# Loading the first K block by partitions (16, then 112) in rows of 64 KB, and writing the last head apart, in a decode attention kernel

## The chip, the cores and the metric

The kernel runs on one core of one Trainium2 chip; the other cores are idle. The metric is the device time of one execution in microseconds (us).

HBM is the chip's main memory and SBUF the core's own, of 128 rows called partitions. A load is issued on the queue of an engine and cut into packets, here one row each, which 16 DMA engines carry side by side (in the kernel before, the first 16 packets all start between 1.74 and 2.10 us).

## The reference

It is one decoding step of grouped-query attention: 32 query heads, 8 K/V heads, one query position, 65,536 keys, head size 128, all in bf16.

```python
B, Hq, Hkv, Sq, Sk, D = 1, 32, 8, 1, 65536, 128

def reference(q, k, v):
    rep = Hq // Hkv                       # 4 query heads share a K/V head
    k = jnp.repeat(k, rep, axis=1)
    v = jnp.repeat(v, rep, axis=1)
    scores = jnp.einsum("bhqd,bhkd->bhqk", q, k) * D ** -0.5
    p = _softmax(scores, axis=-1)
    return jnp.einsum("bhqk,bhkd->bhqd", p, v)
```

K and V are 128 MiB each and every byte is used once, so the kernel is a stream of loads with arithmetic beside it.

## The kernel before

K and V are cut into 16 blocks of 8 MiB each (block i is half of a head). A block lies in SBUF as 128 partitions of 64 KB; partition p holds 256 consecutive keys, a single run of 64 KB in HBM. There are two K buffers and one V buffer. All blocks are loaded on the queue of SP (SyncE), in the order K0, K1, V0, K2, V1, K3, V2, ...

```python
FIRST = (64, 64, 128)     # columns (keys per partition) of the pieces of K0
KLAST = (128, 128)
VLAST = (72, 32, 16, 8)

def src(t, i):
    h, c = divmod(i, C)
    return t[h, c * CK:(c + 1) * CK, :].rearrange("(p t) d -> p (t d)", p=P)

# on SP
def load(buf, t, i, a, b, s):
    sp.dma_start(buf[:, a * D:b * D], src(t, i)[:, a * D:b * D]).then_inc(s, 16)

def load_k(i):
    if i >= NK:                                   # NK = 2 buffers
        sp.wait_ge(tr_s, (i - NK + 1) * G)        # block i-2 transposed
    if i in (0, N - 1):
        for n, a, b in pieces(FIRST if i == 0 else KLAST):
            load(kbuf[i % NK], kf, i, a, b, (first_in if i == 0 else klast_in)[n])
    else:
        load(kbuf[i % NK], kf, i, 0, T, k_in[i % NK])

def load_v(i):
    if i < N - HALVED:
        if i >= 1:
            sp.wait_ge(pv_s, 2 * i)               # products with block i-1 done
        load(vbuf, vf, i, 0, T, v_in)
        return
    # ... the last two V blocks in pieces

load_k(0)
for j in range(1, N + 1):
    if j < N:
        load_k(j)
    load_v(j - 1)
sp.wait_ge(ox_s, 1)
sp.dma_start(of.rearrange("h (a i) -> a h i", a=A), oX).then_inc(o_out, 16)   # all heads
sp.wait_ge(o_out, 16)
```

q (8 KB) is loaded four times, one copy for every 32 partitions, from the queue of ScalarE (ACT), at the same time as the first K loads:

```python
# on ACT
for a in range(A):                                # A = 4
    ac.dma_start(q4[a * S4:(a + 1) * S4, :], qf).then_inc(q_in, 16)
```

VectorE (DVE) waits for q, spreads it, and transposes a K block in 16 pieces; TensorE (PE) makes scores of each piece; ACT moves the scores out of PSUM and takes the exponentials. The products with V block i follow the scores of K block i+1. V1 can be loaded only after K0 and K1 have been transposed, one after the other, and V0 has been used.

## Time and profile before

The median is 628.71 us (6 runs, 628.66 to 628.82).

| Reading | Value | From |
|---|---|---|
| DMA | 9 tenths busy or more in 39 of 40 slices | slices |
| VectorE, TensorE, ACT | 54, 43, 44% busy | busy times |
| packet of 64 KB / 32 KB / 16 KB, one engine | 2.418 / 1.213 / 0.611 us | packet records of the trace |
| block of 8 MiB, steady | 19.35 us | 8 packets of 64 KB on each of 16 engines |

The page's slices of the kernel before (each digit the busy share of a fortieth of the span in tenths, GB/s what the DMA moved):

```profile
span 627.5 us, 20255 instructions
...
DVE  2949176390853908448094470935719367195900
...
DMA  9999999999999999999999999999999999999996
GB/s 368 439 456 414 455 414 455 414 451 414 451 418 451 418 451 418 443 426 434 434 426 439 418 451 409 460 409 460 409 460 409 460 409 460 409 428 434 434 432 276
```

The DMA row is what bounds the kernel: 32 blocks at 19.35 us are 619 us of the 627.5. The packet records, which give the start, length, size and queue of every packet, have no gap to speak of on any of the 16 engines (0.3 us of idle per engine in all) from the first packet at 1.74 us to the end of the last loads at 622.5 to 624.1 us. In such a stream DMA time that is lost is lost for good (below, a first block that lands 19.8 us late ends in a last one 21.3 us late), and work on other engines counts only where it makes the queue run dry (6.2 us in k_whole below).

The windows view of the first 50 us (busy time of each engine in the stretch, then granted clock, DMA share and GB/s; packets of 64 KB make neighbouring stretches uneven, and shares can pass 1):

```profile
core 0: us, PE busy (x) PEld busy (x) DVE busy (x) ACT busy (x) POOL busy (x), PEclk, DMA share, GB/s
0.00:10.00 10.00, 0.00 (x0) 0.00 (x0) 0.29 (x2) 1.49 (x2) 0.67 (x6) 1.00 0.85 331
10.00:20.00 10.00, 2.61 (x73) 2.26 (x74) 7.83 (x15) 1.05 (x5) 0.00 (x0) 1.00 1.06 452
20.00:30.00 10.00, 4.45 (x126) 3.79 (x122) 8.52 (x9) 5.81 (x28) 0.00 (x0) 1.00 1.08 469
30.00:40.00 10.00, 2.46 (x67) 2.03 (x64) 5.74 (x8) 6.86 (x32) 0.30 (x1) 1.00 0.98 420
40.00:50.00 10.00, 2.48 (x68) 2.13 (x69) 6.28 (x6) 4.18 (x14) 0.07 (x1) 1.00 0.97 420
```

Some lines of its timeline (start, length, engine, line, operation, operands; in brackets the idle time before it and what ended it), and how long the q loads took to land, from the view of that tensor:

```profile
12.01 0.24 DVE L290 STREAM_TRANSPOSE scs<-scs 128x64 int32<-128x64 int32 x1 [10.85 <-DMA scs<-in_q_dram]
...
71.19 0.33 SPq L126 DMA_DIRECT2D vbuf<-in_v_dram  x1
...
625.03 0.16 DVE L386 TENSOR_TENSOR oTX<-acc,small 128x4 bf16<-128x4 f32 x1 [11.91 <-PE acc L212]
625.23 0.21 DVE L388 STREAM_TRANSPOSE oTX<-oTX 128x32 bf16<-128x32 bf16 x1
625.47 0.67 SPq L158 DMA_DIRECT2D out_dram<-oTX  x1
...
DMA to landing us min/median/max: 4.1/7.8/9.9
```

VectorE waits 10.85 us for q, not for K. V1 is issued at 71.19 us, while the engines are busy with the block queued before it until 80.0 to 81.8 us, so 8.8 to 10.6 us remain. The tail from the last accumulate at 625.03 us to the end is 2.5 us.

### The profile page before, as it was taken

The page shows a single profiled execution, that of the slowest core. Times are in us where ns is not written, and L with a number is a line of the kernel's source. Part 1 is how long each engine was busy: PE and PEld are TensorE (multiplying, and loading weights), DVE is VectorE, ACT ScalarE, POOL GpSimd, SP SyncE. Part 2 cuts the span into 40 slices and gives each one's busy share as a digit, 9 for nine tenths or more (in the row PEclk, how much of TensorE's full clock was granted, in tenths as well). Part 3 has the DMA queues.
Part 4 walks back from the last instruction along what each step waited for, and adds up shares of the span by engine and source line. Part 5 has one row for each costly group of instructions (what it writes and reads, how often), then busy time and mean ns, then how long its engine had stood idle before and what let it go on. Part 6 is the DMA issues. An engine that isn't in the chain of part 4 may idle for free.

```text
span 627.5 us, 20255 instructions
## 1 busy us (share of the span) xinstructions
PE 267.3 (43%) x8194; PEld 241.6 (39%) x8194; DVE 341.3 (54%) x411; ACT 274.8 (44%) x1178; POOL 10.5 (2%) x32
## 2 busy tenths in 40 slices
PE   0414537154361543615346252462624526146445
PEld 0314426044361433614335152351524525146444
DVE  2949176390853908448094470935719367195900
ACT  0556435164351734517346172451625526264640
POOL 0000000000000000000000000000000000000000
DMA  9999999999999999999999999999999999999996
GB/s 368 439 456 414 455 414 455 414 451 414 451 418 451 418 451 418 443 426 434 434 426 439 418 451 409 460 409 460 409 460 409 460 409 460 409 428 434 434 432 276
DMA packets 6088, 268.53 MB, mean 428 GB/s; under 512 B 964, under 2 KB 964, under 8 KB 1220
## 3 DMA queue, kind: packets, MB, share of 16 engines
q1 hardware_dynamic: 5892, 268.45, 99.1%
q10 hardware_dynamic: 192, 0.03, 0.0%
q8 instruction: 2, 0.03, 0.0%
q14 instruction: 2, 0.02, 0.0%
HBM read 268.47 MB, written 0.01 MB: 428 GB/s over the span
## 4 chain that ended last, share of the span: by engine, by line
DMA 66%; DVE 15%; PE 9%; issue 9%; SPq 1%; DVEq 0%
DMA kbuf<-in_k_dram 58%; DVE ktb L303 14%; PE acc L212 9%; DMA vbuf<-in_v_dram 7%; DVE small L310 1%; PE qkb L203 1%; SPq L126 1%; DVEq L354 0%; DVEq L356 0%; DVE oTX L388 0%; DVE oTX L386 0%; DVEq L385 0%
## 5 line engine op out<-in xcount | busy, mean ns | idle before, releaser
L303 DVE STREAM_TRANSPOSE ktb<-kbuf 128x1024 int32<-128x1024 int32 x256 | 296.0, 1215 | 148.9 <-DMA kbuf<-in_k_dram 148.9
L403 ACT ACTIVATE scs<-qkb 32x64 f32<-32x64 f32 x1024 | 219.5, 214 | 274.9 <-PE qkb L203 263.8
L203 PE MATMUL qkb<-qblk,ktb 128*128 x4096 | 152.2, 175 | 340.3 <-DVE ktb L303 311.0
L203 PEld LDWEIGHTS qkb<-qblk,ktb 128*128 128x128 bf16 x4096 | 129.2, 105 | 363.1 <-DVE ktb L303 363.1
L212 PE MATMUL acc<-pts,vbuf 128*128 128x4 bf16 x4096 | 114.7, 166 | 17.3 <-DMA vbuf<-in_v_dram 12.9
L212 PEld LDWEIGHTS acc<-pts,vbuf 128*128 128x128 bf16 x4096 | 112.0, 104 | 20.1 <-issue 10.6
L310 DVE TENSOR_REDUCE small<-scs 128x4 f32<-128x256 f32 x64 | 36.8, 575 | 61.3 <-ACT scs L403 61.3
L426 ACT ACTIVATE pts<-scs,small 128x256 bf16<-128x256 f32 x64 | 48.9, 853 | 36.8 <-PE acc L212 36.5
L173 POOL PARTITION_ALL_REDUCE small<-small x16 | 5.9, 370 | 588.5 <-DVE small L365 588.5
L426 ACT ACTIVATION_READ_ACCUMULATOR pts<-scs,small 128x1 f32 x64 | 13.7, 214 | 0.0
L372 DVE COPY small<-acc 128x4 f32<-128x4 f32 x8 | 1.3, 163 | 22.7 <-PE acc L212 22.7
L414 ACT ACTIVATE small<-small 128x4 f32<-128x4 f32 x16 | 3.3, 206 | 22.4 <-POOL small L173 22.4
L378 DVE TENSOR_TENSOR small<-acc,small 128x4 f32<-128x4 f32 x7 | 1.1, 162 | 15.7 <-PE acc L212 15.7
L386 DVE TENSOR_TENSOR oTX<-acc,small 128x4 bf16<-128x4 f32 x1 | 0.2, 163 | 11.9 <-PE acc L212 11.9
L290 DVE STREAM_TRANSPOSE scs<-scs 128x64 int32<-128x64 int32 x1 | 0.2, 245 | 10.9 <-DMA scs<-in_q_dram 10.9
L365 DVE TENSOR_REDUCE small<-small 128x4 f32<-128x16 f32 (+1 forms) x16 | 2.9, 184 | 1.3
L165 POOL PARTITION_ALL_REDUCE small<-small x8 | 3.4, 430 | 12.7 <-DVE small L323 12.7
L370 DVE TENSOR_TENSOR small<-small 128x4 f32<-128x4 f32 x8 | 1.3, 163 | 4.0 <-POOL small L173 4.0
L321 DVE TENSOR_TENSOR small<-small 128x4 f32<-128x4 f32 x8 | 1.3, 164 | 3.0 <-ACT pts L426 2.7
L396 ACT ACT_TABLE_LOAD x1 | 1.3, 1283 | 3.0 <-issue 3.0
L381 DVE TENSOR_TENSOR oTX<-small 128x4 f32 x7 | 1.1, 164 | 1.7 <-DVE small L327 1.7
L319 DVE TENSOR_TENSOR small<-small 128x4 f32<-128x4 f32 x8 | 1.4, 180 | 0.9
(18 smaller groups left out, 8.8 us busy)
## 6 DMA issues: line engine op xcount, KB each, us to landing
kbuf<-in_k_dram SPq DMA_DIRECT2D x3, 4096.0 KB, 39.8
vbuf<-in_v_dram SPq DMA_DIRECT2D x3, 4096.0 KB, 24.5
kbuf<-in_k_dram SPq DMA_DIRECT2D x2, 2048.0 KB, 11.0
vbuf<-in_v_dram SPq DMA_DIRECT2D x1, 2304.0 KB, 11.2
vbuf<-in_v_dram SPq DMA_DIRECT2D x1, 1024.0 KB, 13.3
vbuf<-in_v_dram SPq DMA_DIRECT2D x1, 512.0 KB, 14.1
vbuf<-in_v_dram SPq DMA_DIRECT2D x1, 256.0 KB, 14.3
kbuf<-in_k_dram SPq DMA_DIRECT2D x14, 49.4
```

What stands on the lines that cost most here:

```text
L126: sp.dma_start(buf[:, a * D:b * D], src(t, i)[:, a * D:b * D]).then_inc(s, 16)
L165: g.partition_all_reduce(lsum, rhead, P, bass.bass_isa.ReduceOp.add).then_inc(ls_s, 1)
L173: g.partition_all_reduce(mtot if b else mfirst, hmax[:, b * R:(b + 1) * R], P, bass.bass_isa.ReduceOp.max,).then_inc(hma_s, 1)
L203: ins = pe.matmul(o, lhsT=kt[:, be // NE, be % NE, n * P:(n + 1) * P], rhs=q_, start=be == 0, stop=be == NB * NE - 1,)
L212: ins = pe.matmul(acc[:, 0:R], lhsT=vbuf[:, t * D:(t + 1) * D], rhs=pts[:, t * R:(t + 1) * R], start=t == 0, stop=t == T - 1,)
L303: dv.transpose(to.rearrange("p (b t j) -> p b t j", b=NB, t=TG), fr.rearrange("p (t b i) -> p b t i", b=NB, t=TG),).then_inc(tr_s, 1)
L310: dv.tensor_reduce(hp[b][:, u * R:(u + 1) * R], scs[:, u * W:(u + 1) * W].rearrange("p (n g) -> p g n", g=R), AX.X, ALU.max,).then_inc(mx_ ...
L319: dv.tensor_tensor(o2, o1, wgt, ALU.mult).then_inc(ow_s, 1)
L365: dv.tensor_reduce(hmax[:, b * R:(b + 1) * R], hp[b].rearrange("p (u g) -> p g u", g=R), AX.X, ALU.max,).then_inc(hm_s, 1)
L403: ins = ac.activation(to[a * S4:(a + 1) * S4, x, :, :], fr[x * S4:(x + 1) * S4, a, :, :], AF.Copy)
L414: ac.activation(negb[b], mtot if b else mfirst, AF.Copy, scale=-scale).then_inc(nb_s, 1)
L426: ac.activation(pv[:, g_, :], sv[:, g_, :], AF.Exp, bias=negb[b][:, g_:g_ + 1], scale=scale, accum_out=rsum[b][:, g_:g_ + 1],).then_inc(ex ...
```

## The change

The intent is twofold: to read the first K block in whole rows of 64 KB instead of pieces of rows, a small part (16 partitions) first; and to shorten the tail, by writing heads 0 to 27 while the last V loads still run, and the last four with small DMAs on two queues. In the kernel before, VectorE can transpose the first columns of K0 while the rest lands; now it waits for the whole block.

```diff
-FIRST = (64, 64, 128)
+FIRST = (16, 112)
...
+    def out_rows(e, a, h0, h1, s):
+        e.dma_start(of[h0:h1, a * S4:(a + 1) * S4], oX[a * S4 + h0:a * S4 + h1, :]).then_inc(s, 16)
+
+    def last_out(e, half):
+        e.wait_ge(ox_s, 2)
+        for a in range(half * A // 2, (half + 1) * A // 2):
+            out_rows(e, a, Hq - R, Hq, end_s)
...
-            if i in (0, N - 1):
-                for n, a, b in pieces(FIRST if i == 0 else KLAST):
-                    load(kbuf[i % NK], kf, i, a, b, (first_in if i == 0 else klast_in)[n])
+            if i == 0:
+                for n, a, b in pieces(FIRST):
+                    sp.dma_start(kbuf[0][a:b, :], src(kf, 0)[a:b, :]).then_inc(first_in[n], 16)
+            elif i == N - 1:
+                for n, a, b in pieces(KLAST):
+                    load(kbuf[i % NK], kf, i, a, b, klast_in[n])
...
-        sp.wait_ge(ox_s, 1)
-        sp.dma_start(of.rearrange("h (a i) -> a h i", a=A), oX).then_inc(o_out, 16)
-        sp.wait_ge(o_out, 16)
+        last_out(sp, 0)
+        sp.wait_ge(o_out, 16 * A)
+        sp.wait_ge(end_s, 16 * A)
...  # VectorE waits for both pieces before the first transpose of K0
+        dv.wait_ge(fin_s, H - 1)
+        dv.transpose(oX, oT).then_inc(ox_s, 1)
         weigh(H - 1)
         divisor(H - 1)
+        dv.wait_ge(o_out, 16 * A)
...  # ACT, after its last exponential
+        ac.wait_ge(ox_s, 1)
+        for a in range(A):
+            out_rows(ac, a, 0, Hq - R, o_out)
+        last_out(ac, 1)
```

## The prediction

> **What bounds the kernel now.** The DMA stream. The page's slices show DMA 9 tenths busy in every slice but the last; the packet records of the trace show no gap on the 16 engines from 1.7 us to about 623 us. A 64 KB packet takes 2.418 us (16 engines: 433 GB/s), an 8 MB block 19.35 us, 32 blocks 619 of the 627.5 us. VectorE is busy 54%. So time moves only by DMA time lost in the stream, a gap in it, or the tail. The gap nearest to opening is before V block 1: its load waits for the products of block 0, is issued at 71.19 us (timeline of the DMA queue), and the engines finish what is queued before it at 80.6 to 82.2 us: slack 9 to 11 us.
>
> **Rows of 64 KB.** 16 KB packets take 0.611 us, 32 KB 1.213: whole rows save only about 0.15 us. Per-engine lag (four engines 0.3 to 1.8 us late, from start to end) may change by 1 us.
>
> **q comes later.** The four q loads (12 packets per engine with semaphore writes) alternate one by one with K packets. Today those are 16 KB, and q is complete at 11.6 us (VectorE waits until 12.01). With 64 KB packets the same alternation passes about ten of them: q at 27 us or later even if each takes 2.42 us. From q to the issue of V1, in durations of this trace: q copies 1.6, transposes of block 0 19.3, moves and maximum 5.2, transposes of block 1 19.3, last scores and products 8.2; so V1 starts about 54.5 us after q: 82 us. That alone costs 0 to 3 us.
>
> **Sixteen partitions.** [...]
>
> **Tail.** The output write is issued at 625.47, its packets run 626.74 to 627.02. Smaller writes may save 0.1 to 0.3 us; two issues per queue take some back. The other heads' early writes cost at most 0.15 us.
>
> **Prediction.** 645 us, 8 in 10 between 630 and 650. Faster by over 2%: 0.01; within: 0.34; slower: 0.65.
>
> **What would show it.** Packet records:[...] q packets one per K packet, q complete past 40 us; VectorE's first transpose past 42 us; V1's issue at 95 to 100 us after a stretch of idle DMA; later periods of 77.4 us per head unchanged; tail within 0.5 us.
>
> **What would make it wrong.** Packets of 2.42 us from the start[...];[...] q served before the K packets.

The forecast's sum was +16.5 us on 628.71, so 645. Nearly all of it came from the paragraph "Sixteen partitions", whose terms are cut here, as are the signs that went with them: they rested on a supposed mechanism that no trace or run of this case shows; the runs below show how long the packets took, no more. With it the author put the end of K block 0 at 29 to 38 us, q at 43 us and V1 at 98 us. "Fair sharing", as the expectations and the text below call it, was the assumption that engines which meet share a rate and the others keep theirs. The terms that still stand (whole rows, the later q, the tail) came to about +1 us, which would have been about 630.

## The result

The median is 650.99 us (6 runs, 649.87 to 651.60), against 628.71 for the kernel before. The ratio is 1.0351, with a 95% interval of 1.0338 to 1.0365: slower. (Ratios are the mean time of one kernel's fast runs over the mean of the other's of the same rounds, so not quite the ratio of the medians quoted.) The execution profiled took 650.18 us.

The page's slices after:

```profile
span 648.5 us, 20262 instructions
...
DVE  0009777629085471926629184571917538095910
...
DMA  9989999989999999998999999999999999999997
GB/s 171 260 280 441 438 420 388 453 388 453 453 404 437 453 445 396 453 453 388 453 453 420 420 453 449 392 453 453 400 441 453 437 404 453 449 392 445 428 420 324
```

The reader should see two things. The loss sits in the first three slices: 171, 260 and 280 GB/s where there were 368, 439 and 456. And the busy row barely shows it: DMA engines that crawl count as busy. Bytes moved, not busy shares, tell whether a stream is at its rate. The windows view after:

```profile
0.00:10.00 10.00, 0.00 (x0) 0.00 (x0) 0.29 (x2) 1.49 (x2) 0.67 (x6) 1.00 0.94 118
10.00:20.00 10.00, 0.00 (x0) 0.00 (x0) 0.00 (x0) 0.00 (x0) 0.00 (x0) 1.00 0.97 199
20.00:30.00 10.00, 0.00 (x0) 0.00 (x0) 0.00 (x0) 0.00 (x0) 0.00 (x0) 1.00 1.17 317
30.00:40.00 10.00, 0.00 (x0) 0.00 (x0) 0.00 (x0) 0.00 (x0) 0.00 (x0) 1.00 0.93 210
40.00:50.00 10.00, 0.00 (x0) 0.00 (x0) 2.88 (x11) 0.00 (x0) 0.00 (x0) 1.00 0.97 387
```

The timeline and the landing of q after:

```profile
46.97 0.24 DVE L302 STREAM_TRANSPOSE scs<-scs 128x64 int32<-128x64 int32 x1 [45.81 <-DMA scs<-in_q_dram]
...
100.97 0.33 SPq L135 DMA_DIRECT2D vbuf<-in_v_dram  x1
...
646.37 0.16 DVE L405 TENSOR_TENSOR oTX<-acc,small 128x4 bf16<-128x4 f32 x1 [11.95 <-PE acc L224]
646.56 0.21 DVE L407 STREAM_TRANSPOSE oTX<-oTX 128x32 bf16<-128x32 bf16 x1
646.80 0.66 SPq L123 DMA_DIRECT2D out_dram<-oTX  x2
646.81 0.61 ACTq L123 DMA_DIRECT2D out_dram<-oTX  x2
...
DMA to landing us min/median/max: 12.2/31.8/44.8
```

VectorE starts 35 us later, still on q; V1 is issued 30 us later. The tail is 2.2 us (646.37 to 648.55), 0.3 less than before.

From the packet records, the length of the first, second, ... packet of 64 KB on each engine after the change (16 packets in each row; all were 2.42 us from the tenth on):

| Packet | Belongs to | Mean us | Shortest to longest |
|---|---|---|---|
| 1 | 16 partitions | 8.64 | 7.96 to 9.19 |
| 2 | 112 partitions | 5.41 | 5.19 to 6.03 |
| 3 | 112 | 4.73 | 4.67 to 4.91 |
| 4 | 112 | 3.25 | 2.88 to 4.77 |
| 5 | 112 | 3.76 | 3.54 to 4.60 |
| 6 | 112 | 4.52 | 4.19 to 4.87 |
| 7 | 112 | 4.70 | 4.64 to 4.89 |
| 8 | 112 | 4.53 | 4.37 to 4.73 |
| 9 | K1 | 3.15 | 2.67 to 3.65 |

And where the 21.0 us between the two spans appear, by the last engine to finish each block:

| Event, last engine | Before | After | Difference |
|---|---|---|---|
| K0 landed | 23.7 | 43.6 | +19.8 |
| K2 landed (the last block queued before V1) | 81.8 | 102.0 | +20.3 |
| V1 landed | 101.1 | 122.4 | +21.3 |
| last V piece landed | 624.1 | 645.4 | +21.3 |
| end of the span | 627.5 | 648.5 | +21.0 |

### The profile page after: what moved, and what is told of

It reads as the page before. It is cut to its first block, busy times and chain, and to the rows that moved or that the text cites. A ratio compares the mean times of both kernels' runs of the same rounds, so it can differ in the third digit from the quotient of the medians.

```text
span 648.5 us, 20262 instructions
## 1 busy us (share of the span) xinstructions
PE 267.0 (41%) x8194; PEld 241.4 (37%) x8194; DVE 341.1 (53%) x412; ACT 275.6 (42%) x1178; POOL 10.5 (2%) x32
## 4 chain that ended last, share of the span: by engine, by line
DMA 58%; DVE 18%; PE 10%; issue 10%; another core or an unknown queue 2%; ACT 1%; DVEq 0%; SPq 0%; ACTq 0%
DMA kbuf<-in_k_dram 44%; DVE ktb L315 16%; PE acc L224 10%; DMA vbuf<-in_v_dram 7%; DMA scs<-in_q_dram 7%; DVE small L322 2%; PE qkb L215 1%; ACT scs L422 1%; SPq L135 0%; DVEq L369 0%; ACTq L412 0%; DVEq L371 0%; DVE qblk L310 0%; DVEq L355 0%
## 5 line engine op out<-in xcount | busy, mean ns | idle before, releaser
L302 DVE STREAM_TRANSPOSE scs<-scs 128x64 int32<-128x64 int32 x1 | 0.2, 245 | 45.8 <-DMA scs<-in_q_dram 45.8
```

## The experiments

Three questions were open. Is the loss the low DMA rate while K0 is loaded by parts of the partitions (the theory), or the late start of VectorE, which waits for q (rival)? Has the output part a share? And why were even the packets of the second piece nearly all at 4.5 us, where I had expected most at 2.4?

Where a forecast stands before "Rival", it is the theory's.

The timed results in one table. "Gap" is the time that an average engine stood idle between the end of K2 and the first packet of V1; "q" is when VectorE got q; times in us.

| Kernel | Median | Ratio (95%) | K0 landed, last engine | q | V1 issued | Gap |
|---|---|---|---|---|---|---|
| before | 628.7 | | 23.7 | 12.0 | 71.2 | 0 |
| full change | 650.99 | 1.0351 (1.0338 to 1.0365) | 43.6 | 47.0 | 101.0 | 1.3 |
| k_only | 650.53 | 1.0346 (1.0330 to 1.0362) | 44.3 | 47.8 | 101.8 | 1.9 |
| out_only | 628.78 | 1.0001 (0.9987 to 1.0015) | 23.8 | 12.0 | 71.1 | 0 |
| k_parts_qfirst | 650.61 | 1.0347 (1.0331 to 1.0363) | 45.8 | 5.2 | 99.3 | 0 |
| k_parts_qsecond | 649.09 | 1.0321 (1.0305 to 1.0337) | 45.0 | 14.4 | 98.9 | 0.1 |
| k_halves | 649.74 | 1.0335 (1.0319 to 1.0351) | 44.3 | 45.4 | 99.4 | 0 |
| k_whole | 634.96 | 1.0098 (1.0082 to 1.0113) | 23.5 | 31.4 | 85.5 | 6.2 |
| k_whole_qfirst | 630.24 | 1.0023 (1.0010 to 1.0037) | 25.3 | 5.5 | 78.6 | 0 |
| k_whole_qsecond | 630.00 | 1.0019 (1.0006 to 1.0033) | 23.6 | 24.9 | 78.9 | 0.3 |

All gave correct results.

### k_only: the K part alone

The kernel before with the K part of the diff and nothing of the output part:

```diff
-FIRST = (64, 64, 128)
+FIRST = (16, 112)
...
+            if i == 0:
+                for n, a, b in pieces(FIRST):
+                    sp.dma_start(kbuf[0][a:b, :], src(kf, 0)[a:b, :]).then_inc(first_in[n], 16)
```

> The kernel before with only the K part of the change (16 then 112 partitions); output written as before. If the K part is the whole loss: 650.8 to 652 us, about 0.35 above the full change (650.99), because the full change's tail (last accumulate to end) is 2.13 us against 2.48 before. If the split output write has a share in the loss: clearly under 650.

Measured: 650.53 us, 21.8 above before. The K part is the whole loss. That is 0.3 us below the stated range, and the 0.35 us that the full change should be better by is not seen: the runs spread by over 1 us, and the next experiment shows that the shorter tail gains no time.

### out_only: the output part alone

The full change with the old `load_k` and the old waits of VectorE:

```diff
-FIRST = (16, 112)
+FIRST = (64, 64, 128)
...
-            if i == 0:
-                for n, a, b in pieces(FIRST):
-                    sp.dma_start(kbuf[0][a:b, :], src(kf, 0)[a:b, :]).then_inc(first_in[n], 16)
+            if i in (0, N - 1):
+                for n, a, b in pieces(FIRST if i == 0 else KLAST):
+                    load(kbuf[i % NK], kf, i, a, b, (first_in if i == 0 else klast_in)[n])
```

> The kernel before with only the output part of the change. From the two traces: tail 0.35 us shorter, early writes cost at most 0.15: 628.3 to 628.6 us. If the loss comes from the output part (its wait on the early writes, its DMAs beside the last V loads): over 630.

Measured: 628.78 us against 628.72 for before, ratio 1.0001, interval 0.9987 to 1.0015. The output part is neutral, a little above the 628.3 to 628.6 expected. Its tail is shorter in its profile as well (last accumulate at 625.10, end at 627.3, so 2.2 us against 2.5), but the timed runs show no gain. Time and span of each run show where it goes: with the output part (here and in the full change) the time is 1.60 to 1.68 us longer than the profile's span in every run, without it 1.27 to 1.39. What the extra 0.3 us outside the span is, no run shows; a tail should be judged by the time, not by the span.

### k_whole: one load of 128 whole rows

k_only with one piece:

```diff
-FIRST = (16, 112)
+FIRST = (128,)
```

> The kernel before, with the first K block in one load of 128 whole rows of 64 KB. [...] packets of 2.42 us, K block 0 complete at 22 us, q complete near 27 us, V block 1 issued at about 82 us, time 628 to 632 us. Rival (the late q and the late start of VectorE are the loss, not the DMA rate): q at 27 instead of 47 us against 12, so a bit under half of the loss remains: about 638.

Measured: 634.96 us. K0 lands as in the kernel before (23.5 us on the last engine), with nearly every packet after an engine's first at 2.42 us: rows of 64 KB are not slow by themselves, the partial sets of partitions are. But the time missed both expectations. q came at 31.4 us, not 27, and V1 was issued at 85.45 us. The queue had run dry by then, as the windows view of this kernel shows:

```profile
70.00:80.00 10.00, 5.86 (x176) 5.24 (x177) 7.83 (x9) 6.84 (x32) 0.00 (x0) 1.00 0.97 419
80.00:86.00 6.00, 5.42 (x198) 5.26 (x195) 1.12 (x4) 2.50 (x11) 0.37 (x1) 1.00 0.00 0
86.00:100.00 14.00, 5.94 (x160) 5.04 (x160) 13.50 (x13) 9.43 (x40) 0.00 (x0) 1.00 1.09 449
```

There are 6.2 us in which an average engine moves nothing, and the loss in time is 6.2 us. So a late q does cost, through a gap in front of V1. What was too small is the estimate of q's way: I had counted about ten K packets, the records have 11 on nearly every engine (about 12 in the kernel before), and the last engine gets its last q packet 1.8 us after the first engine (30.85 against 29.0 us). V1 follows q by 85.45 - 31.38 = 54.07 us here; 100.97 - 46.97 = 54.00 after the full change.

### k_parts_qfirst and k_parts_qsecond: 16 and 112 partitions with an early q

Both are k_only with the four q loads moved from ACT's queue to SP's: ahead of K0 in the first, between the two pieces of K0 in the second.

```diff
 for n, a, b in pieces(FIRST):
     sp.dma_start(kbuf[0][a:b, :], src(kf, 0)[a:b, :]).then_inc(first_in[n], 16)
+    if n == 0:
+        for x in range(A):
+            sp.dma_start(q4[x * S4:(x + 1) * S4, :], qf).then_inc(q_in, 16)
```

> K by 16 then 112 partitions, but the four q loads are issued on the same queue ahead of K, so that q is complete by about 4 us. [...] K packets still take 8 to 9 and 3 to 5 us, K block 0 complete at about 42 us, the DMA stream still about 20 us behind, time 648 to 651 us. Rival (late q is the loss): 628 to 632 us.

> K by 16 then 112 partitions, with the four q loads on the same queue between the two pieces: q is there at about 12 us, and the stream starts no later. [...] K block 0 complete at 42 to 44 us as in the full change, VectorE starts there, V block 1 is issued at about 96 to 99 us, before the queue runs dry at 100 to 102, so the gap of about 1.3 us goes and the slow K block stays: 648 to 650 us (the k-only kernel: 650.5). If the late q were more than that gap: under 645.

Measured: 650.61 and 649.09 us. With q at 5.2 us instead of 47 the kernel is as slow as ever; the rival falls. In the first, the gap before V1 is gone, but the four q issues hold the SP queue, K starts 1.8 us later (first K issue at 2.57 us instead of 0.74), which is about what the gap was worth. In the second, q costs the stream nothing, and the gap is gone as well: 1.4 us less than k_only. That is about what the gap is worth, but the two intervals overlap, so it is not clear of noise. (Its profile, from which the table's columns come, is of its slowest run, 650.40 us.) In both, VectorE's first transpose of K0 waits for K (46.8 and 46.3 us), so V1 is still late; it only just comes in time, because the queue too is late by 20 us.

### k_halves: 64 and 64 partitions

k_only with two other pieces:

```diff
-FIRST = (16, 112)
+FIRST = (64, 64)
```

> The first K block by partitions 0-63, then 64-127: [...] packets of 4.3 to 4.8 us, K block 0 complete at 36 to 41 us, q at about 45 to 50 us, time 643 to 650 us. Rival (something in the small first piece of 16 rows or the 7 rows per engine of the second): packets of 2.42 us, time about 630.

Measured: 649.74 us. Its windows view:

```profile
0.00:10.00 10.00, 0.00 (x0) 0.00 (x0) 0.29 (x2) 1.49 (x2) 0.67 (x6) 1.00 1.01 211
10.00:20.00 10.00, 0.00 (x0) 0.00 (x0) 0.00 (x0) 0.00 (x0) 0.00 (x0) 1.00 1.03 212
20.00:30.00 10.00, 0.00 (x0) 0.00 (x0) 0.00 (x0) 0.00 (x0) 0.00 (x0) 1.00 1.03 212
30.00:40.00 10.00, 0.00 (x0) 0.00 (x0) 0.00 (x0) 0.00 (x0) 0.00 (x0) 1.00 1.03 211
```

A steady half of the usual rate for 40 us, then normal. There is no small piece here and no row count of 7 per engine, and the loss is the same 21 us. The time fell in the expected range, but packets took 4.9 to 5.1 us and K0 landed at 44.3 us, both later than the 4.3 to 4.8 and 36 to 41 expected. There is also no gap before V1: the whole loss is DMA rate. Nothing is won by two loads of half the partitions: each ran at half the rate of a load of all 128 (211 to 212 GB/s, against 442 in k_whole's stretch from 10 to 20 us).

### k_whole_qfirst and k_whole_qsecond: whole rows and an early q

The same two moves of q applied to the single load of 128 rows.

> One load of 128 whole rows, and q ahead of it on the same queue. [...] K block 0 complete at about 22.5 us, first transpose at about 23, V block 1 issued at about 76 us with the queue still busy: 627.5 to 629 us, the same as before within 0.3%; a little less if the engines' lags at the start are smaller.

> One load of 128 whole rows, then the four q loads on the same queue. [...] no late start of the stream, q complete at about 23 us, first transpose at about 25, V block 1 issued at about 77 to 79 us with the queue still busy until 80: 628.3 to 628.9 us, equal to before within 0.05% or a little below. If whole rows cost something by themselves: 630 or more.

Measured: 630.24 and 630.00 us, both a little worse than expected and worse than before. In the first, K's first issue is at 2.58 us instead of 0.74, and K0 lands 1.6 us later (25.3 against 23.7 us on the last engine): the loss of 1.5. In the second, V1 is issued at 78.92 us, when the fastest engine had 1.0 us of work left; a load's first packet comes 1.0 us after its issue (in the kernel before, K0 is issued at 0.75 us and its first packet starts at 1.74). Engines that ran dry there stood idle for 0.3 us on average, and the block landed 0.7 us later, relative to the one before it, than in the kernel before. In the first, V1 is issued 7.4 us later than in the kernel before although VectorE has q at 5.5 us: it now waits for the whole of K0 (first transpose at 25.98 us). No version beats the kernel before: with 16 KB packets first it lets q pass quickly and loses only about 0.15 us to them, by the estimate of the prediction from the packet times above.

### probe: loads of single sets of partitions

Thirteen loads of rows of 64 KB into V's buffer ahead of the whole kernel, each after the one before has landed.

```python
done = 0
for rows, of_ in PROBES:        # SBUF partitions, rows of HBM
    done += 16
    sp.dma_start(vbuf[rows, :], src(vf, 0)[of_, :]).then_inc(probe_in, 16)
    sp.wait_ge(probe_in, done)
```

> The kernel before with thirteen loads of 64 KB rows put ahead of it, one at a time, into the buffer of V; the time of the whole means nothing, the packets do. [...] 128 rows: 2.42 us a packet. Rows 0-15[...]: 8.5 to 9.7. 16-127 and 0-111[...]: most packets 2.42, some 4.8, mean 2.7 to 3.1 alone. [...] Partitions 0-15 from every eighth row of HBM: as rows 0-15 (8.5 to 9.7); every eighth partition from neighbouring rows of HBM: 4.3 to 4.8. Rival (the HBM side, or the small number of rows): speed follows the HBM rows, or all loads of 16 rows are equally slow.

The author's estimate was about half the rate (4.3 to 4.8 us) for 0-31, 0-63, 64-127, every 8th, and every 2nd of 0-31, and for every 7th 2.42 us on most engines.

From the packet records:

| Partitions | Mean packet, us | GB/s, first packet to last |
|---|---|---|
| 0-127 (the last load; the first gave 2.51 and 380) | 2.50 | 410 |
| 0-15 | 8.51 | 112 |
| 0-31 | 4.97 | 199 |
| 0-63 | 5.05 | 201 |
| 64-127 | 5.03 | 201 |
| every 8th (16 rows) | 4.82 | 187 |
| every 2nd of 0-31 | 4.86 | 196 |
| 16-127 | 4.31 | 230 |
| 0-111 | 4.27 | 238 |
| every 7th from 0 (16 rows) | 4.35 | 199 |
| 0-15, from every 8th row of HBM | 8.56 | 109 |
| every 8th, from rows 0-15 of HBM | 4.73 | 199 |

The windows view over the loads of 0-15, 16-127, 0-63 and the last one of 0-127, each stretch just around its load:

```profile
25.10:34.70 9.60, 0.00 (x0) 0.00 (x0) 0.89 (x7) 0.00 (x0) 0.00 (x0) 1.00 0.89 109
36.60:68.70 32.10, 0.00 (x0) 0.00 (x0) 0.00 (x0) 0.00 (x0) 0.00 (x0) 1.00 0.94 229
115.00:136.00 21.00, 0.00 (x0) 0.00 (x0) 0.00 (x0) 0.00 (x0) 0.00 (x0) 1.00 0.96 200
...
201.90:222.50 20.60, 0.00 (x0) 0.00 (x0) 0.00 (x0) 0.00 (x0) 0.00 (x0) 1.00 0.97 407
```

(An engine's first packet differs from its later ones: 3.05 us against 2.42 in the loads of 0-127, but 4.8 against 5.1 in those of 0-31 and 0-63. Sets of 16 rows have first packets alone.) The rate follows the SBUF side and not the HBM rows (last two rows of the table: 8.56 us for 0-15 whatever the HBM rows, 4.73 for every 8th). Rows 0-31 also show that the engines do not take every 16th row: rows 0-15 would have gone first, at the 8.51 us that they took alone, but the first packets of 0-31 took 4.8 us. A load of all 128 cannot be cut into eight neighbours per engine, though: every 8th partition took 4.82 us a packet, and these loads took 2.42. The expectation failed where it counted: 16-127, 0-111 and every 7th from 0 gave 199 to 238 GB/s and means of 4.27 to 4.35 us, where most packets had been expected at 2.42. All 16 engines were slow. That is the same oddity as in the second piece of the changed kernel, now alone and without q.

### probe2 and probe3: which sets of partitions slow which engines

Each pattern is now loaded three times back to back, into three buffers, so that the second packet of an engine shows the steady rate.

```python
for rows, from_ in PROBES:
    done += 48
    for to in (vbuf, kbuf[0], kbuf[1]):
        sp.dma_start(to[rows, :], src(vf, 0)[from_, :]).then_inc(probe_in, 16)
    sp.wait_ge(probe_in, done)
```

> The kernel before with loads of few 64 KB rows ahead of it, each pattern three times back to back into three buffers, so that the second packet of each engine shows the steady rate; the time of the whole means nothing. [...] Theory B[...]: every 4th of 0-31 at 2.42, but 64-95, and every 9th and 14th, at 3.5 or more. Fair sharing, as the prediction had it: in every 10th four engines at 2.42 and four at 4.8[...]. Checks: every 8th of 0-63 and every 17th[...]: 4.8 to 5.1; rows 0-3[...] 8.5 to 9.7; rows 0-1, and rows 0 and 32[...]: 4.8 to 5.1; rows 0 and 64[...] and one row alone: 2.42.

> As the second probe (each pattern three times; the whole time means nothing), to settle why some patterns slow every engine. [...] Theory C[...]: every 5th (8 rows, one pair): six at 2.42, two at 4.8;[...] from 18 and from 19 every 7th (one pair): fourteen at 2.42[...]. Swaps: what SBUF partitions are written decides:[...] Theory D (the spacing of the HBM rows read makes them slow): the swaps come out the other way round.

Theory A was that two engines which slow each other slow the rest as well, so that every 4th, 9th and 14th would be at 2.42 us, and "from 18" and every 10th slow on all engines. Theory C, made from the second probe, was that a single such pair leaves the rest alone, and that two or more slow every engine; it wanted every 11th, every 15th and "from 20" slow throughout, and in the swaps slow partitions slow and fast ones fast, whatever HBM rows fill them. How many such pairs a pattern has was the author's assumption.

From the packet records, the second packet of each engine:

| Partitions (rows) | Second packets, us |
|---|---|
| every 4th of 0-31 (8); of 64-95 (8) | all 2.42 |
| every 9th (8); every 14th (8) | all 2.42 |
| 0 and 64 (2); 0 alone | 2.42 |
| 0, 1 (2); 0, 32 (2) | 5.12; 4.82 |
| 0-3 (4) | 9.82 to 9.91 |
| every 5th (8) | six 2.42, two 4.75 and 4.83 |
| from 18, every 7th (16) | fourteen 2.42, two 4.82 and 4.83 |
| from 19, every 7th (16) | fourteen 2.42, two 4.82 |
| from 20, every 7th (16) | all 4.93 to 4.94 |
| every 10th (8) | all 4.33 to 4.93 |
| every 11th (8) | all 4.37 to 4.92 |
| every 15th (8) | all 5.12 to 5.13 |
| every 8th of 0-63 (8); every 17th (8) | all 5.12 to 5.13 |
| every 6th (16) | all 5.12 to 5.13 |
| from 0, every 7th, filled from the HBM rows of "from 18" (16) | all 4.93 to 4.94 |
| from 18, every 7th, filled from the HBM rows of "from 0" (16) | fourteen 2.42, two 4.83 |
| every 6th, filled from the HBM rows of "from 18" (16) | all 5.12 to 5.13 |
| from 18, every 7th, filled from the HBM rows of "every 6th" (16) | fourteen 2.42, two 4.83 and 4.84 |
| every 10th, filled from the HBM rows of "every 9th" (8) | all 4.60 to 5.02 |
| every 9th, filled from the HBM rows of "every 10th" (8) | all 2.42 |

The windows view of the third kernel over two of its stretches, "from 18" and then "from 0" filled from the rows of "from 18":

```profile
53.60:68.60 15.00, 0.00 (x0) 0.00 (x0) 0.00 (x0) 0.00 (x0) 0.00 (x0) 1.00 0.58 210
70.30:85.80 15.50, 0.00 (x0) 0.00 (x0) 0.00 (x0) 0.00 (x0) 0.00 (x0) 1.00 0.93 203
```

The GB/s are alike, since in both stretches the slowest engine sets the end; the DMA share tells them apart: 0.58 where fourteen engines finish early, 0.93 where all 16 crawl.

None of the three guesses before the second probe survived it: theory A wanted "from 18" slow on all engines, theory B wanted every 9th and every 14th slow, and fair sharing wanted four engines of every 10th at 2.42. The lengths that theory C wanted then came out in every row of the third probe, and theory D's in none. That is no proof of its rule, since no run shows how many pairs a pattern has.

What the small sets show: partitions 0 and 1 slow each other (5.12 us), 0 and 32 as well (4.82), 0 to 3 fourfold (9.82 to 9.91), while 0 and 64 do not (2.42). What the larger ones show: in three patterns (every 5th; every 7th from 18 and from 19) two engines run at half speed, 4.75 to 4.83 us, and the others do not notice, as fair sharing has it. In the other slow patterns of eight or more rows every engine runs at about half speed (4.33 to 5.13 us), and none keeps 2.42. A shift by one partition is enough: every 7th from 19 has two slow engines, every 7th from 20 has sixteen. The spacing alone does not decide (every 4th, 9th and 14th are all at full speed). Nor does the HBM side (the swaps); in one of the six swaps it shifted the length by up to 0.3 us (every 10th, 4.33 to 4.93 against 4.60 to 5.02). By what mechanism some sets slow every engine, no run shows.

For 112 partitions in runs of seven neighbours per engine (an assumption), engine e writes partition 16 + 7e + s at step s. Steps 2, 3 and 4 are then the patterns "from 18", "from 19" and "from 20, every 7th" of the table: fourteen engines at 2.42 us in the first two, all at 4.93 to 4.94 in the third. In the table of the result, the fast packets are the fourth and fifth (means of 3.25 and 3.76 us), which are steps 2 and 3, and the sixth, step 4, is slow (4.52). The other four steps no probe loaded alone. An estimate from the probe's means, 8.51 us for the piece of 16 and seven times 4.31 for that of 112, ends K0 40.4 us into the span for an average engine, from a first packet at 1.7 us (measured: K0's last packets end at 40.7 to 43.5). It was made after the fact, from the rates of these runs; it shows that the effect is large enough, not more.

## Why the prediction was wrong

The direction, the place of the loss (the loads of part of the partitions) and the verdict (slower by over 2%) were right; the size was not: the author had assumed that only engines which meet slow each other. 645 us was predicted with 630 to 650, and 650.99 was measured: +22.3 us instead of +16.5, 1 us above the range.

- **What bounds the kernel**: right. DMA time lost at the start never came back: K0 landed 19.8 us late on the last engine, and the last V piece 21.3 us late.
- **Whole rows save 0.15 us**: nothing contradicts it, and it is too small to be seen. k_whole, with whole rows of all 128 partitions, lands K0 0.2 us earlier.
- **q comes later**: right in kind. The packets of q and K alternate in the traces, with a whole row of 64 KB as one packet: after the change, for one, 16 q packets start at 20.4 to 22.3 us, where the third packets of the 16 engines end (20.4 to 22.3), and 16 more at 23.6 to 25.8 us, where the fourth end (23.6 to 25.8). The estimate was too low: in k_whole q came at 31.4 us, not 27 (11 K packets passed, not ten, and the last engine lags by 1.8 us), and costs 6.2 us in k_whole, not "0 to 3". In the full change this term is nearly hidden: the queue is as late as VectorE, and the gap is 1.3 us.
- **The first piece of 16 partitions**: right in kind. 8.64 us a packet, where all took 2.42 from the tenth on.
- **The second piece of 112 partitions: this is the step that failed.** The prediction took fair sharing and ended K0 at 29 to 38 us. It ended at 40.7 to 43.5. The assumption that each engine takes seven neighbouring partitions fits the probes (the fast packets are those of steps 2 and 3). Wrong was that the other engines keep their full rate when some meet: every 7th from 20, step 4 of the seven, has all 16 at 4.93 to 4.94 us, and in five of the seven steps the piece's shortest packet took 4.19 us or more. The mean packet of the piece was 4.31 us when loaded alone, where my expectation by fair sharing was 2.7 to 3.1. Over seven packets this is over 8 us for an average engine. The last engine, which fair sharing also slows, and which sets the time, lost about 5.5 us (43.5 against 38), about the amount missing.
- **V1's start**: predicted 98 us; issued at 100.97, first packets at 101.9 to 102.3. It follows q (54.0 us in between), which came at 46.4 instead of 43 because the K packets that it lets pass were slower.
- **Tail**: right within its margin, but there is no gain. It is 0.3 us shorter in the profile; the output part alone is neutral in time (1.0001), because as much is added outside the span.
- **What would show it**: q complete past 40 us (46.4), first transpose past 42 (48.5), idle DMA before V1 (1.3 us) came; slow packets lasted until 43.5 us instead of about 38, and V1's issue missed its window of 95 to 100 us by 1.0. The period stays: V loads at 402.17 and 479.47 us after, 77.3 us apart.

## What to carry to other kernels

Cut a DMA-bound load by columns rather than by partitions: here pieces that did not span all 128 partitions held all 16 engines at about half rate or less (112 GB/s for partitions 0-15, 201 for 0-63, 230 for 16-127, against 410 for all), and in a saturated stream that time is gone (21 us in k_halves and in the full change). How many partitions a piece has does not tell its rate: 16 rows, every 7th from 19, left fourteen engines at 2.42 us, and the same from 20 put all 16 at 4.93 to 4.94. And small loads on another queue waited for about one packet of the big stream per packet of their own: q landed 9.9 us after its issue at the most beside packets of 16 KB, 29.2 us beside packets of 64 KB in k_whole, and 44.8 us in the changed kernel. So what must arrive early should go beside small packets, not beside rows of 64 KB.
